# Score rows in two halves of 288, output sums in single banks, and a last MLP partly taken ahead

## The chip, the cores and the metric

The kernel runs on one core of a Trainium2 chip. A core has a matrix engine (PE, with its weight loads shown apart as PEld), a vector engine (DVE), an activation engine (ACT), GpSimd (POOL) and a queue that issues DMA (SP). Each takes its instructions strictly in the order in which they were built and waits on semaphores. PE writes to PSUM, eight banks of 512 fp32 per partition; DVE and ACT read it, POOL doesn't. The metric is device time of the run in microseconds (us): 852.15 median of three (850.63, 852.15, 852.69).

## What is computed

Top-32 attention on 8 batches of 8 heads (576 rows, head dimension 64), and an MLP mixer on its output:

```python
scores = scale * np.matmul(q, k.transpose(0, 1, 3, 2))
kth = np.partition(scores, -32, axis=-1)[..., -32:-31]
scores = np.where(scores >= kth, scores, -1000000000.0)
attn = softmax(scores)                       # over the last axis
x = heads_side_by_side(attn @ v)             # (8, 576, 512)
h = np.maximum(x.transpose(0, 2, 1) @ w_tok1, 0.0) @ w_tok2   # 576 -> 256 -> 576
u = x + h.transpose(0, 2, 1)
out = u + np.maximum(u @ w_ch1, 0.0) @ w_ch2                  # 512 -> 1536 -> 512
```

## The kernel before

**Tiles.** Two heads are a pair: 32 pairs, four to a batch. In a pair (`pair_ops`) the 576 score rows of each head are worked off in five groups of tiles of 128 rows: groups 0 to 3 hold one tile of either head (two "rows" of work below, n = 2), group 4 the last 64 rows of both heads in one tile (n = 1). That makes 288 tiles of 128 x 576 scores.

**One group** (`unit_ops`, from line 419). PE forms the scores in fp32 (L367 for two tiles, L358 for one) into "big" buffers: four of them, each of two PSUM banks. ACT copies them to SBUF as S (L424). DVE finds a threshold from above: the largest eight of seven segments (L431), then a merge of their candidates (L434, L435, L442), giving `thi`. ACT takes the sign of S against it and counts (L445), POOL multiplies S by that sign into X (L448), DVE puts in markers (L456), and the largest eight of X (L460) give the exact 32nd value, `tlo`. The masked exponentials then come about in one of several forms, chosen for each group by a letter in the table FORMS (a string for each pair in turn, a letter for each group), and for the last pair by `form_of`:
- D: ACT takes the exponentials (L468); POOL alone makes the mask from tlo (nt L470, Z L473, M L476) and multiplies (Pm L479).
- R: ACT takes a relu against tlo (L486), PE adds it, scaled by a huge factor ("sink", L506), to scores that it forms again (L367), and ACT takes the exponentials of the sum (L512).
- A: ACT writes the exponentials to PSUM (L517), DVE compares and multiplies in one instruction (L520).
- Q: as R, with the relu made on POOL. The table before has none.

Pm is transposed by DMA (in the last pair's last two groups by PE and a DVE copy, L531 and L535), multiplied with v on PE ("PV", L390) and normalized by DVE (L408, L409) into Xb. Each of the 32 normalizations fills two heads of a batch.

**The MLP** of a batch (`mlp_ops`) starts when its four pairs are normalized: token sums (L574, L579, relu L584), the second token product with x added through identity matmuls (L595 to L602), copied as UT in four chunks of 128 channels (L608), then twelve inner sums of 128 hidden channels over the four chunks (L617, relu to H2 L623), then output sums of twelve inner products and four identity matmuls for each 128 rows (L635, L640), evicted by ACT two at a time (L648) and stored. For the last batch the first three chunks of UT are formed before the last pair is done; all twelve inner sums wait for the fourth.

**What sets the order.** `Plan` is a list scheduler that runs when the kernel is built. Every piece of work is added with an engine, a duration, a due time, its dependencies and the buffers that it takes (`acq`). Of the work that could start at the same moment the one due first goes first. The due times are multiples of T = 2.45 for each tile plus an offset from the table W, by kind of work. The order that comes out is fixed in the program; on the chip, semaphores alone decide when each instruction starts.

At the end a check of the counters (`check`, L696 to L719) sets a flag, and a slow exact path would run if it were set; it doesn't run here.

Of the kernel before, what the change touches and what calls it, by code (L numbers as in the profile page):

```python
# [19 lines left out]
    T=2.45, ev=1.35, evh=1.4, seg=1.35, t2=1.8, ct=2.8, xm=4.4, dm=3.5, m5=4.2, ex=2.45, tn=2.6,  # L20
    z=6.3, mk=4.95, pm=4.65, rw=3.5, og=5.45, eg=4.9, ea=2.8, st=4.45, tr=3.0, pv=7.2, fin=8.2,
    mlp=10.95, stp=1.05,
)

FORMS = ("DRDAD", "RDADR")
# [9 lines left out]
class Buf:  # L35
    __slots__ = ("tag", "slot", "users", "left", "end", "t")

    def __init__(self, tag):
        self.tag, self.slot, self.users, self.left, self.end, self.t = tag, None, 0, 0, 0.0, None

# [5 lines left out]
class Plan:  # L46
# [10 lines left out]
    def tag(self, name, tiles):  # L57
        self.tags[name] = [[t, 0.0, True] for t in tiles]

# [17 lines left out]
    def run(self):  # L77
# [16 lines left out]
        while len(order) < n:  # L94
# [41 lines left out]
            for b in o.acq:  # L136
                k = None
                for i, s in enumerate(self.tags[b.tag]):
                    if s[2] and (k is None or s[1] < self.tags[b.tag][k][1]):
                        k = i  # L140
                s = self.tags[b.tag][k]
                s[2] = False
                b.slot, b.t = k, s[0]
# [8 lines left out]
            for b in o.use:  # L152
                b.left -= 1
                b.end = max(b.end, done if o.dma else o.end + self.HOP)
                if b.left == 0:
                    s = self.tags[b.tag][b.slot]
                    s[1], s[2] = b.end, True
# [14 lines left out]
def kernel(  # L172
# [51 lines left out]
    identB = sbt("identB", [P, P], bf16)  # L224
# [35 lines left out]
    slots("big", 4, [P, 2, 512], f32, psum=True)  # L260

# [4 lines left out]
    nc.vector.tensor_copy(out=identB[:, :], in_=identF[:, :])  # L266
# [25 lines left out]
    def flat(t):  # L292
        return t[:, :, :].rearrange("p j c -> p (j c)")

    def pair_ops(p):
# [59 lines left out]
        def scores(g, bs, start):  # L355
            if g == 4:
                for lo, hi in ((0, SM), (SM, S)):
                    nc.tensor.matmul(  # L358
                        out=flat(bs[0].t)[:, lo:hi], lhsT=qT.t[:, SM : SM + P], rhs=kT.t[:, lo:hi],
                        start=start, stop=True,  # L360
                    )
                return

            for lo, hi in ((0, SM // 2), (SM // 2, SM), (SM, S)):
                for h in range(2):
                    r = slice(64 * h, 64 * h + 64)
                    nc.tensor.matmul(  # L367
                        out=flat(bs[h].t)[:, lo:hi], lhsT=qT.t[r, g * P : (g + 1) * P],
                        rhs=kT.t[r, lo:hi], start=start, stop=start or hi > SM // 2,
                    )  # L370

        PT = []
        for g in range(5):
            n = 2 if g < 4 else 1
            bs, Ss = [Buf("big") for _ in range(n)], Buf("S")
            i0 = 9 * p + 2 * g
            om = plan.add("PE", 1.25 if g < 4 else 1.1, T * i0, lambda g=g, bs=bs: scores(g, bs, True), [eq, ek], acq=bs + [Ss], use=[qT, kT])
            PT.append(unit_ops(i0, n, bs, Ss, om, p, g, scores, [qT, kT]))
# [35 lines left out]
        nm = plan.add("DVE", 0.86, tv + T, norm, [o], acq=[rd], use=[O, X])  # L414
        mixed.setdefault(b, []).append(nm)

    order_t2 = [None, None]

    def unit_ops(i0, n, s, S_, om, p, g, scores, qkT):
# [5 lines left out]
            out=S_.t[:, h, :], in_=flat(s[h].t)[:, 0:S]), [om], use=[s[h], S_]) for h in range(n)]  # L425
        cts = []
        for h in range(n):
# [3 lines left out]
            segs = [plan.add("DVE", 0.146, th + W["seg"] * T + 0.01 * a, lambda a=a, cd=cd, h=h: nc.vector.max(  # L431
# [6 lines left out]
            a1 = plan.add("DVE", 0.075, tr, m_(2), segs, acq=[m8], use=[cd])  # L438
            a2 = plan.add("DVE", 0.134, tr + .01, c_(2), [a1], use=[cd, m8])
            a3 = plan.add("DVE", 0.097, tr + .02, m_(5), [a2], use=[cd, m8])  # L440
            a4 = plan.add("DVE", 0.156, tr + .03, c_(5), [a3], use=[cd, m8])
# [6 lines left out]
        xm = plan.add("POOL", 0.12 + 1.11 * n, te + W["xm"] * T, lambda: nc.gpsimd.tensor_tensor(  # L448
# [5 lines left out]
        for h in range(n):  # L454
            i, r = i0 + h, NT - 1 - i0 - h
            dm = plan.add("DVE", 0.125, te + W["dm"] * T, lambda h=h, i=i: nc.vector.tensor_scalar(  # L456
# [3 lines left out]
            m = plan.add("DVE", 0.675, te + W["m5"] * T + 0.3 * h * T, lambda h=h, r=r: nc.vector.max(  # L460
# [21 lines left out]
        elif form in ("R", "Q"):  # L482
# [20 lines left out]
            def again():  # L503
                for h in range(n):
                    for lo, hi in ((0, SM), (SM, S)):
                        nc.tensor.matmul(  # L506
                            out=flat(es[h].t)[:, lo:hi], lhsT=sink[:, "RQ".index(form), :], rhs=Wm.t[:, h, lo:hi],
# [3 lines left out]
            og = plan.add("PE", (1.25 if n == 2 else 1.1) + 0.33 * n, te + W["og"] * T, again, ws, acq=es, use=[Wm] + qkT)  # L511
            last = [plan.add("ACT", 0.535, te + W["eg"] * T + 0.2 * h, lambda h=h: nc.scalar.activation(  # L512
                out=Pm.t[:, h, 0:S], in_=flat(es[h].t)[:, 0:S], func=AF.Exp, scale=scale / UP),
# [10 lines left out]
        if p == NPAIR - 1 and g >= 3:  # L524
# [3 lines left out]
            def tp():  # L528
                o = flat(tb.t).bitcast(bf16)
                for j in range(5 * n):  # L530
                    nc.tensor.transpose(  # L531
                        o[:, j * P : (j + 1) * P], Pm.t[:, j // 5, (j % 5) * P : (j % 5 + 1) * P], identB[:, :])
# [5 lines left out]
            return PT, dt  # L538
        dt = plan.add("SP", 0.06, te + 5.4 * T, lambda: nc.sync.dma_start_transpose(
# [4 lines left out]
    def form_of(p, g):  # L544
        if p == NPAIR - 1 and g >= 2:
            return "R" if g == 2 else "A"
        return FORMS[p % len(FORMS)][g]

    def mlp_ops(b):
        X = xb[b]  # L550
        fin = b == B - 1
        base = T * (36 * (b + 1) + (W["fin"] if fin else W["mlp"]))
        H1, UT, H2 = Buf("H1"), Buf("UT"), Buf("H2")
        n = [0.0]
        step = T * W["stp"] if not fin else 1.3
# [8 lines left out]
        for lo, hi in parts:  # L564
# [22 lines left out]
            for cc in range(lo, hi):  # L587
                pb = Buf("big")

                def f(cc=cc, pb=pb):  # L590
# [6 lines left out]
                    for t in range(4):  # L597
                        nc.tensor.matmul(
                            out=o[:, t:SM:4], lhsT=X.t[:, t, ks], rhs=identB[:, :], start=False, stop=(t == 3))
# [9 lines left out]
                    out=UT.t[:, cc, :], in_=flat(pb.t)[:, 0:S]), [o], use=[pb, UT]))  # L609
        h2 = []  # L610
        for fc in range(NF):
            pb = Buf("big")

            def f(fc=fc, pb=pb):
                for lo, hi in ((0, SM), (SM, S)):
                    for cc in range(NC):
                        nc.tensor.matmul(  # L617
                            out=flat(pb.t)[:, lo:hi], lhsT=wc1b[:, cc, fc * P : (fc + 1) * P],
# [3 lines left out]
            o = plan.add("PE", 1.1, d, f, uts + l3, acq=[pb] + ([H2] if fc == 0 else []), use=[UT, H2])  # L622
            h2.append(plan.add("ACT", 0.535, d + 1, lambda fc=fc, pb=pb: nc.scalar.activation(  # L623
                out=H2.t[:, fc, :], in_=flat(pb.t)[:, 0:S], func=AF.Relu), [o], use=[pb, H2]))
        for s0 in (0, 2, 4):
            sn = 2 if s0 < 4 else 1
            r = P if s0 < 4 else ST
            pb, ob = Buf("big"), Buf("ob")
            dep = h2
            for h in range(sn):  # L630
                for part in range(2):
                    def f(part=part, sc=s0 + h, h=h, pb=pb, r=r):
                        cs = slice(sc * P, sc * P + r)
                        for fc in range(6 * part, 6 * part + 6):
                            nc.tensor.matmul(  # L635
                                out=pb.t[0:r, h, 0:C], lhsT=H2.t[:, fc, cs], rhs=wc2b[:, fc, :],
                                start=(fc == 0), stop=False)
                        if part:
                            for cc in range(NC):
                                nc.tensor.matmul(  # L640
                                    out=pb.t[0:r, h, cc * P : (cc + 1) * P], lhsT=UT.t[:, cc, cs], rhs=identB[:, :],
# [4 lines left out]
                                 acq=[pb, ob] if (h, part) == (0, 0) else [], use=[H2, pb] + ([UT] if part else []))  # L646
                    dep = [o]
            e = plan.add("ACT", 0.1 + 0.4 * sn, d + 1, lambda pb=pb, ob=ob, r=r, sn=sn: nc.scalar.copy(  # L648
                out=ob.t[0:r, 0:sn, :], in_=pb.t[0:r, 0:sn, 0:C]), [o], use=[pb, ob])
# [8 lines left out]
            plan.add("SP", 0.06, d + 2, st, [e], use=[ob], dma=1.0)  # L658
# [36 lines left out]
    def check():  # L695
        nc.vector.memset(ones[:, :], 1.0)  # L696

        nc.vector.tensor_scalar(out=ti[:, :], in0=cnt[:, :], scalar1=0.5, scalar2=None, op0=ALU.mult)
        nc.vector.scalar_tensor_tensor(out=tmp[:, :], in0=ti[:, :], scalar=2.0, in1=cnt[:, :],
                                       op0=ALU.mult, op1=ALU.not_equal)  # L700
        nc.vector.tensor_reduce(out=bad[:, 0:1], in_=tmp[:, :], op=ALU.add, axis=AX.X)
        nc.vector.tensor_scalar(out=tmp[:, :], in0=cnt[:, :], scalar1=-521.0, scalar2=None, op0=ALU.add)
        nc.vector.tensor_tensor(out=tmp[:, :], in0=tmp[:, :], in1=tmp[:, :], op=ALU.mult)
        nc.vector.tensor_reduce(out=bad[:, 1:2], in_=tmp[:, :], op=ALU.max, axis=AX.X)
        nc.vector.tensor_scalar(out=bad[:, 1:2], in0=bad[:, 1:2], scalar1=56.0, scalar2=None, op0=ALU.is_gt)
        nc.vector.tensor_tensor(out=tmp[:, :], in0=thi[:, 7:], in1=tlo[:, 7:], op=ALU.is_gt)
        nc.vector.scalar_tensor_tensor(out=tmp[:, :], in0=tlo[:, 7:], scalar=LOW, in1=tmp[:, :],
                                       op0=ALU.is_gt, op1=ALU.mult)
        nc.vector.tensor_reduce(out=bad[:, 2:3], in_=tmp[:, :], op=ALU.min, axis=AX.X)
        nc.vector.tensor_scalar(out=bad[:, 2:3], in0=bad[:, 2:3], scalar1=0.5, scalar2=None, op0=ALU.is_lt)  # L710
        nc.vector.tensor_reduce(out=bad[:, 3:4], in_=bad[:, 0:3], op=ALU.add, axis=AX.X)
# [4 lines left out]
    c1 = plan.add("DVE", 4.4, tc_, check, [order_t2[1], mixed[B - 1][-1]])  # L716
    c2 = plan.add("PE", 0.2, tc_ + 1, lambda: nc.tensor.matmul(
# [186 lines left out]
```

## Time and profile before

| | busy us | share of the span |
|---|---|---|
| PE | 695.2 | 82% |
| DVE | 788.7 | 93% |
| ACT | 754.4 | 89% |
| POOL | 722.5 | 86% |

The profiled execution has a span of 844.1 us at a mean granted PE clock of 0.934. A line of a group gives the line, engine, operation, output and inputs with their shapes, count, then busy us and mean ns of one, then idle time ahead of it and what ended it. Durations of neighbours on one engine overlap by some tens of ns, so the distance from start to start is what one costs. A line of a stretch gives its length and the busy time of each engine in it. PE's busy time is modelled, and an fp32 matmul shows as two records.

### The profile page before, as it was taken

Reading aid. Unit: us, or ns where it says so; the run is one execution under the profiler, and the core shown is the slowest. Engines: PE = TensorE matmul, PEld = TensorE weight load, DVE = VectorE, ACT = ScalarE, POOL = GpSimd, SP = SyncE. Lnnn points to the kernel's source line nnn. Section 1 sums busy time; section 2 is a strip of 40 time slices with the busy share of each in tenths; the row PEclk is TensorE's granted clock in tenths of the full one; section 3 lists DMA queues with packets and bytes.
Section 4 is the critical chain, followed back from the end, with each engine's and each line's share of the span. In section 5 each row is a group of like instructions: output and inputs, shape, how many; then the busy total and the mean of one; then the engine's idle time right before and its main releaser. Section 6 shows DMA issues by size and latency. Waiting matters only on the chain.

```text
span 844.1 us, 20557 instructions
## 1 busy us (share of the span) xinstructions
PE 695.2 (82%) x6055; PEld 473.5 (56%) x6055; DVE 788.7 (93%) x4780; ACT 754.4 (89%) x1428; POOL 722.5 (86%) x557
## 2 busy tenths in 40 slices
PE   6566657789888987899888996889878997789996
PEld 4355445566655655566655565556555665556553
DVE  5999999999999999999999999999999999999840
ACT  6797879999999999999999999999999999999851
POOL 1998989998999989989998998989899999989900
PEclk8686669999899999999999999999999999999998
DMA  5785965565554575367563465546564665425501
GB/s 126 137 140 101 142 109 114 84 123 123 116 113 82 108 154 105 73 104 138 116 134 70 98 140 104 108 89 124 132 111 81 103 138 115 78 56 68 121 12 61
DMA packets 311033, 89.65 MB, mean 106 GB/s; under 512 B 303744, under 2 KB 305664, under 8 KB 310912
## 3 DMA queue, kind: packets, MB, share of 16 engines
q1 hardware_dynamic: 306960, 84.19, 50.8%
q0 software_dynamic: 2752, 3.77, 3.2%
q8 instruction: 49, 0.80, 0.4%
q14 instruction: 72, 0.59, 0.2%
q10 hardware_dynamic: 1200, 0.30, 0.2%
HBM read 35.85 MB, written 9.44 MB: 54 GB/s over the span
## 4 chain that ended last, share of the span: by engine, by line
DVE 29%; POOL 11%; PE 9%; ACT 3%; issue 1%; POOLq 0%; ACTq 0%; DVEq 0%
DVE cd L431 10%; DVE tlo L460 7%; POOL X L448 5%; PE big L635 3%; DVE cd L435 3%; POOL Pm L479 3%; PE big L617 2%; DVE Pm L520 2%; DVE m L434 2%; POOL Z L473 2%; PE big L367 2%; DVE Xb L409 2%; POOL M L476 1%; DVE X L456 1%; DVE thi L442 1%
## 5 line engine op out<-in xcount | busy, mean ns | idle before, releaser
L431 DVE MAX8 cd<-S 128x8 f32<-128x82 f32 (+1 forms) x2016 | 409.4, 231 | 12.1 <-ACT S L424 12.1
L448 POOL TENSOR_TENSOR X<-S,sg 128x1152 f32<-128x1152 f32 (+1 forms) x160 | 343.8, 2165 | 29.6 <-ACT sg L445 28.6
L367 PE MATMUL big<-kT,qT 64*128 64x256 f32 (+1 forms) x1932 | 233.2, 373 | 22.2 <-ACT kT L347 12.2
L445 ACT ACTIVATE sg<-S,thi 128x576 bf16<-128x576 f32 x288 | 226.5, 787 | 23.5 <-DVE thi L442 17.9
L367 PEld LDWEIGHTS big<-kT,qT 64*128 64x128 f32 x1932 | 193.0, 202 | 62.9 <-ACT kT L347 13.6
L460 DVE MAX8 tlo<-X 128x8 f32<-128x588 f32 x288 | 220.2, 764 | 2.5 <-POOL X L448 1.3
L424 ACT COPY S<-big 128x576 f32<-128x576 f32 x288 | 177.3, 648 | 13.2 <-PE big L367 10.8
L479 POOL TENSOR_TENSOR Pm<-E,M 128x1152 bf16<-128x1152 bf16 (+1 forms) x79 | 169.6, 2146 | 6.6
L617 PE MATMUL big<-UT,wc1b 128*128 128x512 bf16 (+1 forms) x768 | 107.0, 290 | 26.9 <-ACT Pm L512 12.3
L473 POOL TENSOR_SCALAR Z<-S,nt 128x576 f32<-128x576 f32 x142 | 105.8, 745 | 13.5
L635 PE MATMUL big<-wc2b,H 128*128 128x512 bf16 (+1 forms) x480 | 111.6, 379 | 3.6 <-ACT Pm L512 2.3
L617 PEld LDWEIGHTS <-wc1b 128*128 128x128 bf16 x768 | 55.3, 99 | 78.2 <-issue 31.1
L434 DVE MAX8 m<-cd 128x8 f32<-128x14 f32 x576 | 98.3, 171 | 0.5
L435 DVE MATCH_REPLACE8 cd<-m,cd 128x14 f32<-128x14 f32 x576 | 98.0, 170 | 0.0
L476 POOL TENSOR_SCALAR M<-Z 128x1152 bf16<-128x1152 f32 (+1 forms) x79 | 82.9, 1049 | 6.8
L468 ACT ACTIVATE E<-S 128x1152 bf16<-128x1152 f32 (+1 forms) x79 | 84.8, 1074 | 1.3 <-POOL Pm L479 0.5
L506 PE MATMUL big<-M,sink 128*128 128x512 bf16 (+1 forms) x162 | 31.6, 302 | 52.4 <-ACT M L486 43.1
L635 PEld LDWEIGHTS <-H 128*128 128x128 bf16 (+1 forms) x480 | 46.0, 100 | 49.9 <-issue 3.3
L358 PE MATMUL big<-kT,qT 128*128 128x64 f32 (+1 forms) x188 | 67.3, 486 | 6.0 <-ACT S L424 4.2
L623 ACT ACTIVATE H<-big 128x576 bf16<-128x576 f32 x96 | 63.4, 669 | 4.2 <-PE big L617 4.2
L390 PE MATMUL big<-vb,PT 128*128 128x65 bf16 x1600 | 58.3, 197 | 7.2 <-DMA PT<-Pm 6.1
L486 ACT ACTIVATE M<-S,tlo 128x576 bf16<-128x576 f32 x81 | 60.7, 785 | 2.7 <-DVE tlo L460 2.3
(78 smaller groups left out, 873.3 us busy)
## 6 DMA issues: line engine op xcount, KB each, us to landing
qL<-in_q_dram SPq DMA_DIRECT2D x64, 128.0 KB, 2.9
vL<-in_v_dram SPq DMA_DIRECT2D x64, 128.0 KB, 2.9
out_dram<-ob SPq DMA_DIRECT2D x16, 512.0 KB, 3.2
kL<-in_k_dram SPq DMA_DIRECT2D x62, 128.0 KB, 2.9
PT<-Pm SPq DMA_TRANSPOSE x158, 3.5
wc1b<-in_moe_w_ch_dram POOLq DMA_DIRECT2D x4, 384.0 KB, 5.2
wc2b<-in_moe_w_ch_dram POOLq DMA_DIRECT2D x4, 384.0 KB, 6.7
qL<-in_q_dram SPq DMA_DIRECT2D x64, 16.0 KB, 2.4
```

The source lines that it names most:

```text
L367: nc.tensor.matmul(out=flat(bs[h].t)[:, lo:hi], lhsT=qT.t[r, g * P : (g + 1) * P], rhs=kT.t[r, lo:hi], start=start, stop=start or hi > SM ...
L424: evs = [plan.add("ACT", 0.525, t + W["ev"] * T + W["evh"] * h * T, lambda h=h: nc.scalar.copy(out=S_.t[:, h, :], in_=flat(s[h].t)[:, 0:S] ...
L431: segs = [plan.add("DVE", 0.146, th + W["seg"] * T + 0.01 * a, lambda a=a, cd=cd, h=h: nc.vector.max(cd.t[:, a, :], S_.t[:, h, bounds[a] : ...
L434: m_ = lambda n_, cd=cd, m8=m8: (lambda: nc.vector.max(m8.t[:, :], cd.t[:, :, 0:n_]))
L435: c_ = lambda n_, cd=cd, m8=m8: (lambda: nc.vector.match_replace(cd.t[:, :, 0:n_], m8.t[:, :], cd.t[:, :, 0:n_], NEG))
L445: cts.append(plan.add("ACT", 0.77, th + W["ct"] * T, lambda h=h, i=i, r=r: nc.scalar.activation(out=sg.t[:, h, :], in_=S_.t[:, h, :], func ...
L448: xm = plan.add("POOL", 0.12 + 1.11 * n, te + W["xm"] * T, lambda: nc.gpsimd.tensor_tensor(out=X.t[:, XW - S : XW - S + n * S].rearrange(" ...
L460: m = plan.add("DVE", 0.675, te + W["m5"] * T + 0.3 * h * T, lambda h=h, r=r: nc.vector.max(tlo[:, r : r + 8], X.t[:, h * XW : (h + 1) * X ...
L473: zs = [plan.add("POOL", 0.835, te + W["z"] * T + 0.01 * h, lambda h=h: nc.gpsimd.tensor_scalar(out=Z.t[:, h, :], in0=S_.t[:, h, :], scala ...
L479: last = [plan.add("POOL", 0.12 + 1.11 * n, te + W["pm"] * T, lambda: nc.gpsimd.tensor_tensor(out=Pm.t[:, 0:n, 0:S], in0=E.t[:, 0:n, :], i ...
L617: nc.tensor.matmul(out=flat(pb.t)[:, lo:hi], lhsT=wc1b[:, cc, fc * P : (fc + 1) * P], rhs=UT.t[:, cc, lo:hi], start=(cc == 0), stop=(cc == ...
L635: nc.tensor.matmul(out=pb.t[0:r, h, 0:C], lhsT=H2.t[:, fc, cs], rhs=wc2b[:, fc, :], start=(fc == 0), stop=False)
```

## The change

Five things change together.

1. *Halves of 288.* Score rows, the sums of form R and the MLP's inner sums no longer lie at 0 to 575 of a two-bank buffer (512 + 64, in fp32 256 + 256 + 64), but at 224 to 799, so that 288 fall into either bank and each half is one matmul.
2. *Single banks.* The MLP's output sums take one bank each ("one", half of a "big", with a rule in the planner which half to give) and are evicted one by one.
3. *Forms and due times.* FORMS has four strings in place of two, a table LAST gives those of the last two pairs, and most of W is new, with values of their own for the last but one batch's MLP.
4. *The last batch's MLP* (`mlp_tail`): the inner sums over the first three chunks of UT are taken ahead and copied to SBUF buffers that are free by then (q, k, v, E, Z, kT); x is added to the output sums first, by identity matmuls. When the fourth chunk is there, each of the twelve inner sums needs two more matmuls, a DVE add of the part taken ahead, and a relu by ACT; five output sums in three "big" buffers take in each hidden chunk as it comes.
5. *The check* is thirteen pieces for the planner instead of one.

```diff
-    T=2.45, ev=1.35, evh=1.4, seg=1.35, t2=1.8, ct=2.8, xm=4.4, dm=3.5, m5=4.2, ex=2.45, tn=2.6,
-    z=6.3, mk=4.95, pm=4.65, rw=3.5, og=5.45, eg=4.9, ea=2.8, st=4.45, tr=3.0, pv=7.2, fin=8.2,
-    mlp=10.95, stp=1.05,
+    T=2.45, ev=-0.8, evh=0.45, seg=2.15, t2=3.1, ct=1.2, xm=3.65, dm=3.2, m5=3.25, ex=3.95, tn=3.15,
+    z=6.0, mk=0.8, pm=3.85, rw=4.55, og=6.55, eg=2.8, ea=1.95, st=4.25, tr=0.35, pv=7.65, fin=8.2,
+    mlp=15.75, stp=1.95, mlq=13.3, stq=0.85, hp=7.35, hps=1.55,
...
-FORMS = ("DRDAD", "RDADR")
+FORMS = ("DRDAD", "RDADA", "DRDRD", "RDDRA")
+
+LAST = ("DRRDR", "QAADA")
...
+    plan.split("one", "big")
+
+    HS = S // 2
+    L0 = 512 - HS
...
+    def row(t):
+        return flat(t)[:, L0 : L0 + S]
...
-            for lo, hi in ((0, SM // 2), (SM // 2, SM), (SM, S)):
+                for h in range(2):
...
-                        out=flat(bs[h].t)[:, lo:hi], lhsT=qT.t[r, g * P : (g + 1) * P],
-                        rhs=kT.t[r, lo:hi], start=start, stop=start or hi > SM // 2,
+                        out=row(bs[h].t)[:, lo:hi], lhsT=qT.t[r, g * P : (g + 1) * P],
+                        rhs=kT.t[r, lo:hi], start=start, stop=True,
...
-        if p == NPAIR - 1 and g >= 2:
-            return "R" if g == 2 else "A"
+        if p >= NPAIR - 2:
+            return LAST[p - NPAIR + 2][g]
...
+        if fin:
+            return mlp_tail(b, base, UT, H2, uts)
...
+                pb = Buf("one")
...
-            e = plan.add("ACT", 0.1 + 0.4 * sn, d + 1, lambda pb=pb, ob=ob, r=r, sn=sn: nc.scalar.copy(
-                out=ob.t[0:r, 0:sn, :], in_=pb.t[0:r, 0:sn, 0:C]), [o], use=[pb, ob])
+                es.append(plan.add("ACT", 0.48, d + 1, lambda pb=pb, ob=ob, r=r, h=h: nc.scalar.copy(
+                    out=ob.t[0:r, h, :], in_=pb.t[0:r, pb.half, :]), [o], acq=[ob] if h == 0 else [], use=[pb, ob]))
...
+    def mlp_tail(b, base, UT, H2, uts):
...
+        for fc in range(NF):
+            pb = Buf("big")
+            B_, half = parts[fc]
+            d = base - T * W["hp"] + W["hps"] * T * fc
+            dep = uts[0 : NC - 1] + l3 + (late_d if B_.tag in ("E", "Z") else [])
+            o = plan.add("PE", 0.78, d, lambda fc=fc, pb=pb: hidden(pb, fc, range(NC - 1)), dep,
+                         acq=[pb] + ([H2] if fc == 0 else []) + ([B_] if half == 0 else []), use=[UT, H2, B_])
+            ready.append(plan.add("ACT", 0.525, d + 0.1, lambda fc=fc, pb=pb: nc.scalar.copy(
+                out=part(fc), in_=row(pb.t)), [o], use=[pb, B_, H2]))
+
+        outs = [Buf("big"), Buf("big"), Buf("big")]
...
+        r1 = plan.add("PE", 1.8, d - 0.5, lambda: residual(range(NC - 1)), uts[0 : NC - 1] + l4, acq=outs, use=[UT])
...
+        for fc in range(NF):
+            pb = Buf("big")
...
+            o = plan.add("PE", 0.28, d, lambda fc=fc, pb=pb: hidden(pb, fc, (NC - 1,)), uts + [ready[fc]],
+                         acq=[pb], use=[UT, H2])
...
+            a = plan.add("DVE", 0.7, d + 0.3, lambda fc=fc, pb=pb: nc.vector.tensor_tensor(
+                out=part(fc), in0=row(pb.t), in1=part(fc), op=ALU.add), [o, ready[fc]], use=[pb, B_])
+            relus.append(plan.add("ACT", 0.53, d + 0.6, lambda fc=fc: nc.scalar.activation(
+                out=H2.t[:, fc, :], in_=part(fc), func=AF.Relu), [a], use=[B_, H2]))
+            if fc < NF - 2:
+                def f(fc=fc):
+                    for t in range(5):
+                        outer(t, fc)
+
+                prev = plan.add("PE", 1.09, d + 1.5, f, [relus[-1], prev], use=[H2] + outs)
```

## The prediction

> **What bounds the kernel now.** I read the page first (busy times and slices), then busy time by stretch, the waits of VectorE (DVE), the groups by shape, and last the end of the run in order of time.
>
> ```profile
> PE 695.2 (82%) x6055; PEld 473.5 (56%) x6055; DVE 788.7 (93%) x4780; ACT 754.4 (89%) x1428; POOL 722.5 (86%) x557
> DVE  5999999999999999999999999999999999999840
> ```
> ```profile
> 100.00:790.00 690.00, 589.49 (x5258) 401.01 (x5259) 683.84 (x4155) 653.44 (x1246) 635.67 (x483) 0.96 0.55 107
> ```
> ```profile
> 790.00:807.40 17.40, 14.28 (x180) 9.94 (x176) 14.46 (x55) 11.32 (x21) 10.77 (x8) 1.00 0.45 97
> 807.40:837.00 29.60, 28.39 (x200) 14.66 (x199) 4.29 (x15) 11.42 (x17) 0.00 (x0) 1.00 0.10 37
> 837.00:844.10 7.10, 0.00 (x0) 0.00 (x0) 0.00 (x0) 0.01 (x1) 0.00 (x0) 0.60 0.11 27
> ```
>
> A row holds stretch and length, then the busy time of PE, PE's weight loads, DVE, ACT, POOL. There are two regimes. From 100 to 790 us DVE is busy 683.8 of 690 us (6.2 us idle), ACT has 36.6 us of idle and POOL 54. From 807.4, the end of the last normalization, DVE and POOL have nothing left but the counters' check, and PE works alone through the last batch's channel MLP; 7.1 us of output and exit follow. The chain of what ended last shows that tail:
>
> ```profile
> 806.61 0.83 DVE Xb L409
> 809.94 12.00 PE big L617 x96
> 822.06 2.70 PE big L635 x12
> 833.42 2.71 PE big L635 x12
> ```
>
> So the time is (DVE work up to the last normalization) + (DVE's idle) + (tail). I price the change in these three.
>
> **What the Trainium skill says.** (1) "Perfetto Trace Analysis", Identifying the Most-Contended Engine: the engine of highest occupancy is the one to relieve, and for VectorE occupancy is a fair measure. The trace agrees: 99.1% for 690 us, with few waits. The same page (Optimization Strategy) warns that regimes differ, which the tail shows. (2) "TensorE: Matmul & The Clock Gate", LDWEIGHTS: a weight load takes its column count over 1.2, an estimate of 107 ns for 128 columns, so a 64-column matmul cannot cover one. The trace has 98 to 101 ns for bf16 and 187 for fp32. (3) "VectorE: DVE Perf Modes", the perf-mode tier table: a two-tensor op in fp32 or with a PSUM operand runs at one element a cycle. The trace agrees for the nearest row, 804 ns for 576 elements (L520), and I price the new add with it.
>
> **Part 1: the forms.** Each group's top-32 mask is applied in one of several forms, and the tables FORMS and LAST choose. Counting rows (two for a full group, one for the fifth): before A 65, R 81, D 142; after A 52, R 93, D 141, Q 2.
>
> ```profile
> L520 DVE SCALAR_TENSOR_TENSOR Pm<-S,tlo,big 128x576 bf16<-128x576 f32 x65 | 52.1, 804 | 0.4 <-ACT big L517 0.2
> L486 ACT ACTIVATE M<-S,tlo 128x576 bf16<-128x576 f32 x81 | 60.7, 785 | 2.7 <-DVE tlo L460 2.3
> L512 ACT ACTIVATE Pm<-big 128x576 bf16<-128x576 f32 x81 | 49.2, 655 | 7.1 <-PE big L367 4.2 <-PE big L358 2.9
> L517 ACT ACTIVATE big<-S 128x576 f32<-128x576 f32 x65 | 41.9, 675 | 1.4 <-DVE Xb L409 1.2 <-DVE m L434 0.2
> ```
>
> Durations overlap the next instruction by about 0.1 us, so I take distances start to start: L520 0.71, L486 0.67, L512 0.54, L517 0.57 us. DVE loses 13 x 0.71 = **9.2 us**, all on the path. ACT: -13 x 0.57 + 12 x 1.21 + 1.1 (the Q exps) - 0.5 (one D row) = +7.7; evicting the output sums bank by bank (0.48 each against about 0.9 a pair) adds 0.9. That lies in ACT's idle, which falls from 36.6 to about 19 us, as the stretch itself gets 9 us shorter. POOL is unchanged within 0.3 us (63 full and 15 single D groups against 63 and 16, plus one Q at 2.9).
>
> **Part 2: halves of 288.** A score group is 8 fp32 records of 288 columns in place of 12 (256, 256, 64), of which the 64-column ones sit behind 187 ns loads. 12 records took 1.28 us; I expect 1.0 to 1.2 and take 1.1. The 161 such groups become 175 (more R and Q), the 47 single ones of 1.29 us become 33, so PE loses some 30 us of 695. The inner sums go from 1.00 us (12.00 / 12) to 0.96. PE isn't the bound before 807 us, so this is worth nothing directly: DVE's work hides it. It shortens the wait of ACT's evictions for PE (10.8 us in the run), which helps ACT stay ahead. The single-bank output sums likewise free PSUM sooner, at no path cost.
>
> **Part 3: due times.** The table W reorders all queues. The profile cannot price this. DVE's added idle lies between 0 and 11 us: the stretch 100 to 200 us has 2.58 idle of 100, which over 680 us would be 17.5, less the 6.2 there are. With ACT at 97% in place of 95% I take **+2**.
>
> **Part 4: the last pair.** Before, its last two groups are both A, and DVE finishes them at once. After, the forms are Q A A D A, so the group before the last goes through POOL once its tlo is known. A D chain on POOL is in the timeline:
>
> ```profile
> 792.09 0.19 POOL L470 TENSOR_SCALAR nt<-tlo 128x2 f32<-128x2 f32 x1
> 792.37 1.57 POOL L473 TENSOR_SCALAR Z<-S,nt 128x576 f32<-128x576 f32 x2
> 794.03 1.15 POOL L476 TENSOR_SCALAR M<-Z 128x1152 bf16<-128x1152 f32 x1
> 795.26 2.37 POOL L479 TENSOR_TENSOR Pm<-E,M 128x1152 bf16<-128x1152 bf16 x1
> ```
>
> That is 5.54 us. PE's ten transposes 0.78, their copy 0.82, twenty PV matmuls 0.8, reciprocal and normalization 1.07 and hops 0.3 make 9.3 us from the last full tlo to the end, of which DVE works 3.65 (tlo, mask, copies, normalization). Idle 5.65, and 1.2 before it, while POOL multiplies X (sign 0.8 + X 2.4 + hops, against 2.4 us of DVE work in the built order). 6.9 against 2.9 idle in 790 to 807.4 now: **+4**. The twelve three-chunk sums and their copies to SBUF (PE 0.72, ACT 0.53 each, 9 us) lie beside this chain: they need only the first three chunks of UT, and in PE's queue they stand ahead of the last PV, so they cost nothing if UT is ready some 9 us earlier; up to 3 us if not.
>
> **Part 5: the tail.** Now: from normalization to the last output sum's eviction 807.43 to 837.0, 29.6 us. After: up to UT's fourth chunk as now, 3.2 us. Then twelve rounds of two matmuls (0.24 issue, 0.40 to the result), DVE add (0.78), ACT relu (0.65), and five output matmuls (5 x 0.213 = 1.07). Three of the four PSUM buffers hold output sums, so all rounds share one: round k+1 waits for add k. In PE's queue the sums of round k+2 stand behind the outputs of k, which wait for relu k. The ring over two rounds is 0.40 + 0.78 + 0.65 + 1.07 + three hops of 0.06 = 3.08, so 1.54 us a round, where PE alone would need 1.31. The last round starts at 5 x 3.08 + 1.3 = 16.7, its way to relu takes 2.0, the ten last output matmuls 2.2: 20.9, plus 0.3 for check pieces between adds and 0.6 for the eviction. 3.2 + 20.9 + 0.9 = 25.0: **-4.6** (-7 if PE sets the pace, -2.5 at 1.7 a round). All five outputs, 1.15 MB, now leave at the end, against 128 KB behind a 512 KB one: **+0.5** (0 to 1.5).
>
> **Sum.** -9.2 + 2 + 4 - 4.6 + 0.5 = -7.3 us; 852.15 - 7.3 = **845 us**.
>
> **Rivals.** *Everything hides*: POOL reaches the last D group early enough that DVE still has work (part 4 costs 0), PE paces the tail (-7), no added idle: -9.2 - 7 + 0.5 = -15.7, 836.5 us. For it: POOL's 54 us of slack. Against: in the built order only 1.9 us of DVE work (tlo, mask, one copy) is left behind that tlo. *Given back as waits*: ACT, with half its slack, evicts S late; +7 idle, tail at 1.7: -9.2 + 7 + 4 - 2.5 + 1 = 0.3, 852.5 us. For it: ACT then is as full as DVE was; its idle now is mostly waiting for thresholds (sg on thi, 14.9 us), slack of order, not of work. Against: DVE waits for ACT's S only 12.1 us, nearly all at the start. *A new bound, slower*: the order loses as much as in 100 to 200 us (+11) and the copies delay PV by 3: -9.2 + 11 + 4 + 3 - 4.6 + 0.5 = +4.7, 857 us. For it: every queue is strictly in order and each due time moved. Against: engine loads stay below DVE's.
>
> **How the numbers follow.** Forecast 0.58, everything hides 0.14, given back 0.14, slower 0.14. Bounds are 0.3% = 2.6 us: faster takes the first two less 0.01, 0.71; same 0.15; slower 0.14. The range runs from 838 (just short of the best case) to 853.5 (past the given-back case); the slower case and the far end of the best are left out.
>
> **What would show it.** the mask op of form A x52; DVE at 98.5 to 99% between 100 and 780 us; last normalization near 804.6 (807.4 - 9.2 + 2 + 4, rounded); an idle DVE of 5 us or so ahead of the last PT copy, released by PE after POOL's Pm; adds 1.5 us apart in the tail; PE below 670 us. It is wrong if DVE waits for S above 15 us in the body, if adds follow at 1.3 or 1.8 us, or if PV waits for the ahead sums' copies.

## The result, and the profile after

The changed kernel takes **860.56 us** (859.91 to 861.39) against 851.87 beside it: ratio 1.0104, 95% interval 1.0086 to 1.0121. It is slower by about 1%; 845 us was forecast, and the range of 838 to 853.5 misses it. The granted PE clock is not the reason: at a mean of 0.931 a run of the changed kernel has a span of 858.1 us, and five runs of the kernel before at the same clock, in the round of the halves alone below, have 845.6 to 847.5.

The first page of the changed kernel, busy time and DVE's slices:

```profile
PE 698.7 (81%) x5458; PEld 445.9 (52%) x5495; DVE 795.4 (93%) x4783; ACT 766.4 (89%) x1465; POOL 723.4 (84%) x557
DVE  5999899998999999999999999999999999999852
```

Busy times by stretch: body, last pair up to the end of the last normalization (822.65), tail, output and exit (columns as before: length, then PE, PE's weight loads, DVE, ACT, POOL):

```profile
100.00:790.00 690.00, 580.25 (x4694) 375.38 (x4727) 666.70 (x4052) 650.45 (x1254) 624.37 (x473) 0.95 0.54 106
790.00:822.65 32.65, 31.40 (x305) 20.60 (x307) 24.25 (x111) 25.11 (x47) 19.93 (x15) 1.00 0.38 83
822.65:849.60 26.95, 22.81 (x117) 8.74 (x117) 15.11 (x30) 10.37 (x16) 0.00 (x0) 1.00 0.03 9
849.60:858.90 9.30, 0.00 (x0) 0.00 (x0) 0.00 (x0) 0.01 (x1) 0.00 (x0) 0.58 0.33 112
```

DVE, which was to lose work, idles 23.3 us of the 690 in place of 6.2. The ledger of the two profiles: up to the last normalization DVE's busy time goes from 784.4 to 780.3 us (-4.1) and its idle from 23.0 to 42.4 (start -3.2, body +17.1, last pair +5.5), which puts it 15.2 us later. The tail is 2.6 us shorter, output and exit 2.2 us longer. Together +14.8 between spans of 844.1 and 858.9; the medians differ by 8.7, as the profiled execution of the kernel before was a short one (845.9 us).

Three whole batches late in the run, between last normalizations of a batch, suffer less from that. First the kernel before, then the changed kernel:

```profile
428.14:721.24 293.10, 252.75 (x2264) 171.79 (x2262) 291.17 (x1775) 279.94 (x534) 269.66 (x205) 0.97 0.55 110
```
```profile
434.77:731.29 296.52, 249.87 (x2039) 162.83 (x2052) 289.54 (x1771) 283.66 (x548) 269.92 (x205) 0.96 0.55 109
```

DVE's work falls by 1.6 us and its idle rises from 1.9 to 7.0, so three batches take 3.4 us longer in these two profiles. Other runs below have the same DVE queue in this stretch: 293.0 us (halves alone) and 294.5 (the kernel before without copies of V) with that of before, 296.5 (old end) and 296.7 (without copies of V) with that of the changed kernel. So a batch is 0.7 to 1.2 us longer.

What DVE waits for between 100 and 790 us (us in all, times, longest), before and after:

```profile
DVE rd L408 <- PE big L390: 3.1, 4, 1.5
DVE tlo L460 <- POOL X L448: 0.2, 1, 0.2
```
```profile
DVE cd L478 <- ACT S L471: 8.9, 16, 2.5
DVE rd L454 <- PE big L436: 8.2, 9, 2.4
DVE tlo L507 <- POOL X L495: 1.2, 5, 0.3
```

Before, DVE didn't wait for ACT's copies of S in this stretch (its waits for S, 12.1 us, all lie in the start); after, it waits 8.9 us for them, and 8.2 for PV in place of 3.1. The groups that the forecast rested on, after:

```profile
L413 PE MATMUL big<-kT,qT 64*128 64x288 f32 x1400 | 250.0, 478 | 45.5 <-ACT kT L394 31.8 <-DVE Pm L567 7.7 <-ACT qT L394 3.1
...
L559 ACT ACTIVATE Pm<-big 128x576 bf16<-128x576 f32 x95 | 56.7, 654 | 16.9 <-PE big L413 16.9
...
L567 DVE SCALAR_TENSOR_TENSOR Pm<-S,tlo,big 128x576 bf16<-128x576 f32 x52 | 40.9, 804 | 1.7 <-ACT big L564 1.0 <-DVE tlo L507 0.2
```

The mask of form A is there 52 times at 804 ns, as forecast. But over the whole run PE now waits 31.8 us for the copy of kT (12.2 before), and ACT 16.9 us ahead of form R's exponentials (7.1).

### The profile page after: what moved, and what is told of

Its sections match the earlier page's. It is cut to its first block, busy times and chain, and to the rows that moved or that the text cites. A ratio compares the mean times of both kernels' runs of the same rounds, so it can differ in the third digit from the quotient of the medians.

```text
span 858.9 us, 19498 instructions
## 1 busy us (share of the span) xinstructions
PE 698.7 (81%) x5458; PEld 445.9 (52%) x5495; DVE 795.4 (93%) x4783; ACT 766.4 (89%) x1465; POOL 723.4 (84%) x557
## 4 chain that ended last, share of the span: by engine, by line
DVE 42%; ACT 23%; PE 20%; issue 6%; POOL 5%; DMA 3%; SPq 1%; ACTq 0%; DVEq 0%; POOLq 0%
DVE cd L478 15%; DVE tlo L507 11%; ACT sg L492 8%; PE big L413 6%; PE big L688 6%; ACT S L471 5%; DVE cd L482 5%; DVE Pm L567 3%; DVE m L481 3%; ACT M L533 2%; ACT Pm L559 2%; POOL X L495 2%; DVE thi L489 2%; DVE X L503 2%; PE big L768 2%
## 5 line engine op out<-in xcount | busy, mean ns | idle before, releaser
L413 PE MATMUL big<-kT,qT 64*128 64x288 f32 x1400 | 250.0, 478 | 45.5 <-ACT kT L394 31.8
L413 PEld LDWEIGHTS big<-kT,qT 64*128 64x128 f32 x1400 | 151.6, 214 | 106.6 <-ACT kT L394 34.5
L688 PE MATMUL big<-wc2b,H 128*128 128x512 bf16 (+1 forms) x401 | 99.7, 387 | 13.2 <-ACT S L471 5.9
L668 PE MATMUL big<-UT,wc1b 128*128 128x288 bf16 x672 | 91.2, 286 | 13.7 <-ACT H L674 5.4
L481 DVE MAX8 m<-cd 128x8 f32<-128x14 f32 (+1 forms) x576 | 97.4, 170 | 0.3
L482 DVE MATCH_REPLACE8 cd<-m,cd 128x14 f32<-128x14 f32 (+1 forms) x576 | 97.4, 169 | 0.0
L553 PE MATMUL big<-M,sink 128*128 128x288 bf16 x190 | 39.4, 313 | 43.6 <-ACT M L533 27.8
L559 ACT ACTIVATE Pm<-big 128x576 bf16<-128x576 f32 x95 | 56.7, 654 | 16.9 <-PE big L413 16.9
L533 ACT ACTIVATE M<-S,tlo 128x576 bf16<-128x576 f32 x93 | 69.7, 783 | 2.2 <-DVE tlo L507 2.0
L436 PEld LDWEIGHTS <-PT 128*128 128x128 bf16 x1600 | 54.9, 100 | 15.2 <-issue 7.1
```

The costliest lines, as they stand in the source:

```text
L413: nc.tensor.matmul(out=row(bs[h].t)[:, lo:hi], lhsT=qT.t[r, g * P : (g + 1) * P], rhs=kT.t[r, lo:hi], start=start, stop=True,)
L436: nc.tensor.matmul(out=o[:, g, :], lhsT=src[:, (5 * h if g < 4 else 0) + j, :], rhs=vb.t[:, j, h, :], start=(j == 0), stop=(j == 4),)
L481: m_ = lambda n_, cd=cd, m8=m8: (lambda: nc.vector.max(m8.t[:, :], cd.t[:, :, 0:n_]))
L482: c_ = lambda n_, cd=cd, m8=m8: (lambda: nc.vector.match_replace(cd.t[:, :, 0:n_], m8.t[:, :], cd.t[:, :, 0:n_], NEG))
L668: nc.tensor.matmul(out=row(pb.t)[:, lo:hi], lhsT=wc1b[:, cc, fc * P : (fc + 1) * P], rhs=UT.t[:, cc, lo:hi], start=(cc == 0), stop=(cc == ...
L688: nc.tensor.matmul(out=pb.t[0:r, pb.half, :], lhsT=H2.t[:, fc, cs], rhs=wc2b[:, fc, :], start=(fc == 0), stop=False)
```

## The experiments

All ratios are to the kernel before, timed on the same chip, with 95% intervals. In the expectations TensorE is PE and ScalarE ACT.

**The score rows alone.** `before` with the halves of 288 in scores, R's sums and inner sums; planner inputs and all queues' order as before.

```diff
-            for lo, hi in ((0, SM // 2), (SM // 2, SM), (SM, S)):
+            for lo, hi in ((0, HS), (HS, S)):
```

> The kernel before with halves of 288 for scores, R sums and inner sums, and nothing else: the planner gets the durations and due times of before, so every queue keeps its order. If the halves cause the loss (their matmuls or their evictions across two banks are slower): 860 us. If only the order of the queues does (my theory): 848 to 852 us, a little below before, since a group of scores takes 1.22 us in place of 1.28 and DVE hides it.

847.56 us, 0.9975 [0.9961, 0.9990], just under the range named; PE's busy time is 677.0 in place of 695.2. The halves help by a quarter of a per cent and are not what costs.

**Due times and forms of before in the changed kernel**: W, then FORMS (LAST kept), then both. The planner keeps the changed kernel's durations in all three.

```diff
-FORMS = ("DRDAD", "RDADA", "DRDRD", "RDDRA")
+FORMS = ("DRDAD", "RDADR")
```

> The changed kernel with the due times W of before (those only the new kernel has keep their values; the last but one batch's MLP gets the times of the others). Due-time theory: DVE's idle between 100 and 790 us goes back from 23 us to 10 or less and the time falls by 12 us or more, to 848 or below. Forms theory (more R, so PE and ACT are late): within 3 us of 860.

> The changed kernel with the two strings of FORMS of before for the pairs 0 to 29 (LAST stays): form A goes back from 52 rows to about 60. Forms theory: the idle of DVE falls by more than the 6 us of work that come back, so 850 to 855. Due-time theory: the work comes back and the idle stays, 862 to 868 us.

> The changed kernel with W and FORMS of before; left of the change are halves, single banks, the last two pairs' forms and the last batch's MLP ahead. If due times or forms are the cause: near 850 us, the tail's small gain (the stretch from the last normalization to the end took 36.3 us against 36.7) and the longer last pair (5 us) apart. If the halves or single banks are the cause: 858 or above.

874.53 (1.0284 [1.0251, 1.0316]), 875.37 (1.0290 [1.0254, 1.0327]) and 875.56 us (1.0307 [1.0274, 1.0340]). The first two lie outside every range named for them. Setting back the due times, the forms or both doesn't bring the time back: each is slower by another 1.8 to 2.0% of the time before. These runs don't price the two, though, since each of them also has another order, and the third keeps the new durations beside the halves, the single banks and the end.

**The order, with no instruction changed.** In `before`, one offset of W (seg) moves by 0.1; in the other run only the planner's durations are set to the changed kernel's, such as

```diff
-        nm = plan.add("DVE", 0.86, tv + T, norm, [o], acq=[rd], use=[O, X])
+        nm = plan.add("DVE", 0.97, tv + T, norm, [o], acq=[rd], use=[O, X])
```

> The kernel before with one due time moved by 0.245 us (seg 1.35 to 1.45): the same instructions, in another order on every queue. If any order but the one that was searched out loses (fragile order): slower by 1 to 3%, 858 to 875 us, with DVE's idle between 100 and 790 us well above 6 us. If the order as such doesn't matter: within 3 us of before.

> The kernel before, its planner given the durations of the changed kernel (scores 1.2 for 1.25, X multiply 2.42 for 2.34, DVE pieces longer by 2 to 11 hundredths): again the same instructions in another order. Fragile order: 858 to 875 us. Otherwise within 3 us of before, or a little faster if the new durations fit the chip better.

852.30 us (1.0023 [1.0010, 1.0036]) and **871.12 us (1.0269 [1.0212, 1.0325])**. The second runs the same instructions as before in another order. Its three late batches:

```profile
440.09:743.19 303.10, 255.16 (x2231) 173.27 (x2255) 294.48 (x1772) 280.47 (x535) 270.69 (x205) 0.96 0.55 107
```

Ten us more than before for three batches of the same work; DVE idles 8.6 us. Its busy time grows too, by 3.3: neighbouring instructions overlap by about 0.1 us where the queue runs on, and not where it stops (what else the new sequence does to the overlap wasn't separated). The first run, 0.2% slower, is within the 3 us of the theory that the order doesn't matter: a small shift of one due time is no sure test of it.

**Single banks, and the end, each on top of the halves.** First the output sums in single banks; then LAST, `mlp_tail` and the pieces of the counters' check.

```diff
+                pb = Buf("one")
```
```diff
+        if fin:
+            return mlp_tail(b, base, UT, H2, uts)
```

> Halves of 288 as in the run of halves alone, and output sums in single banks with the new rule for giving buffers; W, FORMS and the end as before. If single banks as such cost (more instructions, another use of PSUM): above 855 with ACT and PE waiting at the output sums. Fragile order: slower too, but with DVE waiting for S and tlo anywhere. If single banks help as meant: 845 or below.

> Halves of 288, and the end of the changed kernel: LAST for the last two pairs, three chunks of the inner sums ahead, check in pieces. The order up to some 760 us is that of halves alone (847.6 us). If the end as I priced it is right apart from its two mis-sized terms: last pair +5, tail -2.6, exit +2.2, so 850 to 855. If the end is what made the body slow: above 860.

855.25 us (1.0061 [1.0042, 1.0079]) and 858.51 (1.0093 [1.0065, 1.0121]), 0.9 and 1.2% above the halves alone. With single banks the last normalization ends 4.6 us later than with the halves alone (811.9 against 807.3), and from there to the end it takes 42.3 us against 36.8. The timeline of the single banks near the end shows where:

```profile
837.18 1.46 PE L678 MATMUL big<-wc2b,H 128*128 128x512 bf16 x6 [0.67 <-ACT ob L691]
838.48 0.39 PE L683 MATMUL big<-identB,UT 128*128 128x128 bf16 x4
838.70 1.46 PE L678 MATMUL big<-wc2b,H 128*128 128x512 bf16 x5
840.19 0.58 ACT L691 COPY ob<-big 128x512 f32<-128x512 f32 x1 [3.06 <-PE big L678]
840.83 1.46 PE L678 MATMUL big<-wc2b,H 128*128 128x512 bf16 x6 [0.67 <-ACT ob L691]
```

Each output sum waits in its middle for the eviction of the one before it, and they follow every 3.65 us, where the halves alone take 2.81. The eviction itself waits too: the identity matmuls (L683) complete a sum, but ACT's copy (L691) is released only by the first six matmuls of the next one (L678), so neighbouring sums take turns. Why the copy waits for them wasn't tried.

With the new end, 858.51 lies between the two ranges named. The last normalization ends 6.1 us later than with the halves alone, and from there to the end it takes 6.2 us more (43.0 us). This is not the end as the changed kernel has it, where that last stretch takes 36.2 us: from the planner inputs of before, the planner put three of the twelve sums that were to be taken ahead behind UT's fourth chunk, which is copied at 816.1. One of the three, and the add behind it:

```profile
830.23 0.64 ACT L710 COPY Z<-big 128x576 f32<-128x576 f32 x1 [0.56 <-PE big L698]
...
831.85 0.76 DVE L746 TENSOR_TENSOR E<-big,E 128x576 f32<-128x576 f32 x1 [2.90 <-PE big L698]
```

**Forms alone, and with due times, on top of the halves.**

```diff
-FORMS = ("DRDAD", "RDADR")
+FORMS = ("DRDAD", "RDADA", "DRDRD", "RDDRA")
```

> The kernel before with the halves of 288 and, beside that, only the changed kernel's table FORMS (the last pair's rule, due times, durations, output sums and end stay as before): A rows 65 to 50, R rows 81 to 96, D rows 142 as before. If DVE's work alone sets the time, 15 rows x 0.71 us = 10.7 us come off the 847.6 us of the halves alone: 837. If the order that the planner makes of the new list decides, the order of due times that fitted the old forms no longer fits, DVE's idle between 100 and 700 us rises from about 6 to 12 to 30 us, and the time lies between 840 and 870 us, without a fixed relation to the 10.7.

> As the run with halves and the new FORMS, with the changed kernel's due times W as well, but the planner's durations, the output sums and the end as before. If the new due times fit the new forms by themselves, it is faster than the run with FORMS alone and near 840 to 848 us. If due times fit only the whole list they were made for, durations and output sums included, it is no better than the run with FORMS alone, 855 to 880 us, with DVE waiting for S or for PV 15 us or more.

**883.01 us (1.0386 [1.0351, 1.0422])** and 865.82 (1.0173 [1.0136, 1.0209]). The first is my Part 1 by itself, with 15 A rows fewer. Its three late batches:

```profile
444.80:752.57 307.77, 260.81 (x2047) 163.25 (x2059) 293.76 (x1753) 285.67 (x543) 271.54 (x206) 0.93 0.54 105
```

DVE has 22 instructions fewer than before in this stretch and is 14.0 us idle in it. Its time lies above even the 840 to 870 us that the second theory allowed. The new due times win 17 us back, so they fit the new forms better than the old ones do, but not nearly to the 840 to 848 us of the first theory for that run; both theories were too simple.

**Durations set back in the changed kernel.**

```diff
-        nm = plan.add("DVE", 0.97, tv + T, norm, [o], acq=[rd], use=[O, X])
+        nm = plan.add("DVE", 0.86, tv + T, norm, [o], acq=[rd], use=[O, X])
```

> The changed kernel with the planner's twelve changed durations set back; every instruction stays, only their order changes. If the order is the cause and W was made for these durations, it is slower than the changed kernel, 865 to 885 us, with DVE's idle between 100 and 790 us above 23 us. If the order matters little here, it stays within 3 us of 860.6.

881.59 us (1.0361 [1.0326, 1.0395]). Due times, durations and forms fit one another: taken one by one, each set of before is worse in the changed kernel, the durations of after are worse in the kernel before, and the forms of after are worse on the halves. The changed kernel loses 1% although its sets fit one another better than any mix that was run.

**The old end in the changed kernel.**

```diff
-        if fin:
-            return mlp_tail(b, base, UT, H2, uts)
```

> The changed kernel with the end of before: the last pair's forms by the old rule (R A A for its last three groups), the last batch's MLP as in the other batches, no sums ahead, the counters' check in one piece; the queue of DVE is the same for its first 3400 of 4241 instructions. By my prices of parts 4 and 5 (+4, -4.6, +0.5) the end is worth nothing either way, and this stays within 2 us of 860.6. If the end costs what it cost with the halves alone (11 us more than the halves alone), it comes to 848 to 852. If the end pays in the changed kernel (its tail is 2.6 us shorter), 862 or more.

857.05 us (854.36 to 861.04), 1.0076 [1.0051, 1.0102]. It lies in none of the three ranges named. The interval overlaps the changed kernel's 1.0086 to 1.0121: the end may cost 2 or 3 us, and there is no sign that it pays. In the profiles the last normalization ends 11.1 us later with the new end (822.7 against 811.6) and the rest is 4.7 us shorter. But some 5 us of the 11.1 are there before the queues of the two differ (at about 755 us), so they are the spread between executions; about 6 us come with the last pair's new forms and the sums taken ahead. The body stays slow without it (three late batches 296.52 us, to the hundredth as in the changed kernel).

**Which wait?** My theory was then that the late copies of kT hold PE, and PV and S behind it. In these runs only the order of ACT's queue is altered, after the planner is done: the copies ahead, back, ahead with the halves alone, and ahead with the old end.

```diff
     order = plan.run()
+    for o, e in early:
+        e.start = min(e.start, o.end + 0.05)
+    order.sort(key=lambda o: (o.start, o.n))
```

> The changed kernel; after the planner is done, each copy of qT and kT to SBUF is moved ahead in ScalarE's queue to where its transposes end (44 copies move, by 1 to 6 places); all other queues stay word for word. If TensorE's waits for kT cause DVE's idle: kT waits of TensorE from 31.8 to below 12 us, DVE's idle between 100 and 790 us from 23 to 12 to 17 us, 850 to 855 us. If the idle comes with the new list of instructions, TensorE waits elsewhere, DVE's idle stays at 20 us or more, and the time within 3 us of 860.6.

> The kernel before with the copies of qT and kT moved back by up to three places in ScalarE's queue where what follows allows it (39 places); all other queues stay. If late copies of kT cause idle in DVE: TensorE's waits for kT from 12 to 25 us or more, DVE's idle between 100 and 790 us from 6 to 12 us or more, 856 to 865 us. If they are slack: 850 to 853 us.

> The halves alone with the copies of qT and kT moved ahead as in the changed kernel with early copies. DVE's idle between 100 and 790 us is 6 us with the halves alone, so at most some 3 us are to be had: 845 to 848 us if kT waits matter; 847.6 or slower, to 852, if the copies moved ahead delay the signs behind them, which DVE's sums wait for.

> The changed kernel with the end of before (857.0 us) and the copies of qT and kT moved ahead. If both effects add up: what the early copies save in the changed kernel comes off again, 846 to 852 us. If the idle comes with the new list of instructions: 855 us or more.

879.04 us (1.0334 [1.0309, 1.0360]), 859.25 (1.0114 [1.0085, 1.0142]), 852.36 (1.0027 [1.0005, 1.0049]) and 874.50 (1.0300 [1.0257, 1.0343]). **The theory didn't hold:** in the first, DVE's idle between 100 and 790 us rose to 38.8 us, where 12 to 17 were expected. Waits of the changed kernel with early copies:

```profile
PE big L416 <- ACT S L474: 28.2, 12, 4.7
DVE cd L481 <- ACT S L474: 25.9, 27, 7.9
...
DVE rd L457 <- PE big L439: 13.3, 9, 2.2
```

Scores (here L416) wait for kT only 0.7 us now, and 28.2 us for ACT's copies of S (2.9 in the changed kernel): what was moved ahead delayed what DVE needs. The edit trades one wait for another, so it doesn't show what the wait for kT costs by itself. Moving the copies back in the kernel before costs 1.1% as well; DVE's waits for PV go from 3.7 to 9.5 us in it. With the halves alone the early copies cost half a per cent. What these runs do show is how much an order is worth: moving the copies of qT and kT in one queue, every other queue the same, makes a kernel 0.5 to 2.3% slower, whichever way they move.

**Or ACT's load?** 26 copies of V are left out (PV then uses earlier values), the same in both kernels.

```diff
-        ov = plan.add("ACT", 0.6, t0 + 4 * T, lambda: nc.scalar.copy(
+        ov = plan.add("ACT", 0.6, t0 + 4 * T, lambda: None if p >= 6 else nc.scalar.copy(
```

> The changed kernel without the copies of V to bf16 from pair 6 on (26 ScalarE copies of 0.74 us; PV then uses the values of earlier pairs, so part of the computation is left out); all queues otherwise as they were. 26 x 0.64 us start to start is 17 us of ScalarE in 640. If ScalarE's load makes DVE wait: DVE's idle between 100 and 790 us from 23 to 8 to 14 us, 847 to 853 us. If the order as such does it, the waits stay: idle 20 us or more, 857 to 861 us.

> The kernel before without the copies of V to bf16 from pair 6 on (part of the computation is left out), all queues otherwise as they were. DVE's idle between 100 and 790 us is 6 us, so at most 3 us are to be had whatever the cause: 848 to 852 us. A gain of 6 us or more would say that ScalarE's load cost the kernel before time that doesn't show as DVE's idle.

856.86 us (1.0062 [1.0038, 1.0087]) and 850.48 (0.9996 [0.9979, 1.0013]). Of the 8 to 14 us that this theory asked for there are some 4, none of them late in the run, and DVE's idle between 100 and 790 us is still 21.8 us. Three late batches of the changed kernel without the copies:

```profile
432.34:728.99 296.65, 252.34 (x2039) 164.08 (x2052) 289.53 (x1771) 277.73 (x536) 269.13 (x205) 0.95 0.54 109
```

ACT has 5.9 us less to do than in the changed kernel, and the stretch is as long as there (296.52). ACT's load doesn't set the length of these batches.

## Why the prediction was wrong

**Part 3, due times: here it failed.** "The profile cannot price this. DVE's added idle lies between 0 and 11 us" and "I take +2". The body alone added 17.1 us (+13.9 with the start). The size depends on the execution: over the profiles with the DVE queue of before (5.9 to 9.4 us idle) and of the changed kernel (19.5 to 23.3, one of them with another queue in the last 24 us) it lies between 10 and 17. I took the bound from the worst stretch of the kernel *before*, which is the idle of an order that fits its list, and says nothing of an order that doesn't. The run with new durations alone shows what an order by itself can do: 2.7% for the same instructions. How much of the idle the new W made, and how much the new list would have in any order, isn't separated: with the W of before the changed kernel is slower still. "DVE at 98.5 to 99% between 100 and 780 us" came out at 96.6%.

**Part 1, forms: "DVE loses 13 x 0.71 = 9.2 us, all on the path".** The count and the 804 ns held, but DVE's busy time fell by 4.1 us only: in the new sequence, with its stops, less of the overlap between neighbours is left. With the forms alone (on the halves) DVE had 15 instructions fewer up to the last normalization and was busy for 788.2 us, before for 784.4. And "all on the path" was no property of DVE: that run took 31.6 us *more* time than before. This is the second step that failed. ACT's idle in the body, which I had fall to about 19 us, rose from 36.6 to 39.6: ACT had its slack, and it was no protection.

**Part 2, halves: right in direction, sizes off.** In the timelines, first before, then after, a group of two tiles takes

```profile
450.76 1.30 PE L367 MATMUL big<-kT,qT 64*128 64x256 f32 x12
```
```profile
442.81 1.24 PE L413 MATMUL big<-kT,qT 64*128 64x288 f32 x8
```

so eight records save 0.06 us on twelve, where 0.18 was priced (1.28 to 1.1). PE's busy time isn't "below 670": 677.0 with the halves alone, and 698.7 with the rest, of which more R groups are a part. "The single-bank output sums likewise free PSUM sooner, at no path cost" is wrong where it was tried alone: 0.9% over the halves alone, with a wait of 0.67 us in each of the last sums.

**Part 4, last pair: about right.** DVE is idle 8.4 us in the last 17.4 us before the end of the last normalization, 6.9 forecast. The timeline shows the wait for POOL's D chain and one more:

```profile
818.67 0.82 DVE L582 COPY PT<-big 128x1280 bf16<-128x1280 bf16 x1 [3.81 <-PE big L578]
821.62 0.22 DVE L454 RECIPROCAL rd<-big 128x10 f32<-128x10 f32 x1 [2.13 <-PE big L436]
```

The 2.13 us belong to the last PV, which stands behind the sums taken ahead in PE's queue: "they cost nothing if UT is ready some 9 us earlier; up to 3 us if not" was decided the wrong way. That PV waits behind the sums taken ahead is close to one of the signs of being wrong that were named; of the other two, DVE's waits for S stay under "15 us in the body", and the adds below come nearer to the forecast 1.5 us than to 1.8.

**Part 5, tail: mis-sized.** The adds:

```profile
835.11 0.76 DVE L784 TENSOR_TENSOR vL<-big,vL 128x576 f32<-128x576 f32 x1 [0.79 <-PE big L736]
836.85 0.76 DVE L784 TENSOR_TENSOR E<-big,E 128x576 f32<-128x576 f32 x1 [0.99 <-PE big L736]
838.40 0.76 DVE L784 TENSOR_TENSOR E<-big,E 128x576 f32<-128x576 f32 x1 [0.79 <-PE big L736]
```

They alternate between some 1.55 and 1.75 us apart, 1.64 in the mean of all twelve against 1.54; the tail wins 2.6 us, not 4.6, near the end of "-7 if PE sets the pace, -2.5 at 1.7 a round". The add was priced by the Trainium skill's "VectorE: DVE Perf Modes", perf-mode tier table (one element a cycle with an operand in PSUM). The trace agrees on the rate: the add takes 0.76 us for 576 elements, a product of 288 fp32 elements in the counters' check (L851, operands in SBUF) 0.46, so 288 more cost 0.30 us or 1.04 ns each, and a cycle is 1.04 ns at the 0.96 GHz of that page's Specifications. The rest, 0.16 us, doesn't grow with the length in these two. The burst of outputs cost 2.2 us, not 0.5: the last store is issued at 851.8, 2.2 us after its eviction, behind four others.

**The rivals.** The slower one, 857 us, came nearest, and the runs bear out its reason, "every queue is strictly in order and each due time moved"; I gave it 0.14. That its sum comes so near is in part luck: it has -9.2 us of DVE's work where -4.1 was measured, and +0.5 for the outputs in place of 2.2. What I held against it, "engine loads stay below DVE's", was true (ACT 94% of the body) and no argument. *Given back as waits* was right in one part too: DVE's new waits for S in the body. The Trainium skill's "Perfetto Trace Analysis", Identifying the Most-Contended Engine, says to optimize the engine of highest occupancy first. The run with the forms alone differs: that engine had fewer instructions to run, and the time rose by 3.9%.

**What stays open.** That an order alone, with no instruction changed, makes idle and loss of this size is shown (new durations in the kernel before, old ones in the changed kernel, the copies moved in ACT's queue). That it is the order that costs the changed kernel its 1%, and not a tie between PE, ACT and DVE that its list of instructions has in any order, is not shown: a search for due times that fit the new list better wasn't tried. Which waits give the changed kernel its 98.8 us a batch is open as well; moving the copies of kT ahead doesn't cure it, and ACT's load doesn't set it. Of all versions run, the halves alone are the fastest, 847.56 us, and the only one that is faster than before.

## What to carry to other kernels

Where a planner writes a strict order and its offsets were fitted to one list of instructions, a changed list may get an order that doesn't fit: allow for a loss (0.2 to 3.9% here) that can be more than the work removed from the fullest engine, and get the bound from runs with shifted planner inputs, not from the idle of the fitted order. Bring in first what leaves every queue as it is; here that part was the whole gain. An edit that removes a long wait is not yet a gain: make it alone, and look at what the instructions that were passed over are waited for.

## What the runs showed of the hardware

- DVE's busy time depends on the order of its queue: the same instructions up to the last normalization are 784.4 us busy in the kernel before and 790.7 with the new durations, whose queue also stands idle longer (23.0 and 42.2 us).
- Two fp32 halves of 288 columns are hardly cheaper than 256 + 256 + 64: 1.24 us a group of two tiles against 1.30, with a median of 187 ns for each fp32 weight load in both.
- An fp32 add on DVE with one operand in PSUM takes 0.76 us for 576 elements a partition, an fp32 product of 288 in SBUF 0.46: 1.04 ns an element and 0.16 us beside.
